# Reordering the last K loads, sharing slots and laying one weight block on 64 partitions in a decode attention kernel

## The chip, the cores and the metric

The kernel runs on one core of a Trainium2 chip. The metric is the time of one execution in microseconds on the device; the figure for a kernel is the median of its runs. Profiles give the "span" of one execution, which is about 2 us shorter than the time. Five engines matter here: PE (matmuls), DVE (transposes and copies), ACT, POOL, and SP, which only issues transfers. The transfers themselves run on 16 DMA engines.

## The reference

One decode step of attention over a KV cache, plus a gated feed-forward part. Cut to what matters:

```
x: 4 x 1 x 1024;  k_cache, v_cache: 4 x 32 x 8192 x 128 (bf16);  wo: 4096 x 1024
q = x @ wq
p = softmax(q @ k_cache^T * Dh**-0.5);  o = p @ v_cache
a = o.reshape(4, 1, 4096) @ wo
out = g * a + (1 - g) * b        # b: feed-forward part; g: a sigmoid gate
```

The caches are 537 of the 576 MB that are read. Everything else is small.

## The kernel before

The caches are read in 64 K pieces and 64 V pieces, each of 4 MB: one transfer to 128 partitions of 32 KB. They go through a ring of five slots, together with the weights. K0 to K63 are followed by the V pieces with a lag of four: K60, V56, K61, V57, and so on. A K piece is transposed on DVE and multiplied on PE; after every fourth, the softmax of a group runs; then four V pieces are multiplied with its result. At the end, wo is read in blocks of 512 rows (1 MB), wo0 to wo7, and multiplied with the heads' outputs (LT). In the profiles, `piece` is a slot of the ring, `o_ps` the product with V, and `acc` the sum to which the wo blocks are added.

```python
ring = ctx.enter_context(tc.tile_pool(name="ring", bufs=5))
def slot():
    return ring.tile([P, RING], BF, name="piece", tag="piece")       # 128 x 32 KB

def wo_piece(g0, g1, r0=0, r1=FR):                                    # a slot for each block
    w = slot()[:, :ng * nr * D].rearrange("p (g r n) -> p g r n", g=ng, r=nr)
    nc.sync.dma_start(out=..., in_=wov[:, g0:g1, r0:r1]...)           # 128 partitions x 8 KB
    def use(): ...  mm_acc(acc[...], LT[:, r0 + r, g0 + g, :], w[:, g, r, ...])
    return use

for u in range(NT + LAG):                                             # NT = 64, LAG = 4
    if u < NT: k_piece(u)
    if u >= LAG: v_piece(u - LAG)
    ...
    if u == NT: o_rows(0, GE); add_x()
    if u == NT + LAG - 2:                                             # after V62
        for g in range(2): wo_piece(g, g + 1)()                       # wo0, wo1
last = [wo_piece(g, g + 1) for g in range(2, NWB - 1)]                # wo2 .. wo6, after V63
last += [wo_piece(NWB - 1, NWB, 0, FR - 1), wo_piece(NWB - 1, NWB, FR - 1, FR)]   # wo7 in two
# ... cuts: V63 is read in four transfers of 1 MB
```

## Time and profile before

| | before |
|---|---|
| time, median (range) | 1351.51 us (1351.25 to 1352.2) |
| span of the profiled run | 1349.4 us |
| DMA engines, mean over the span | 427 GB/s |
| PE busy / DVE busy | 79% / 46% |
| last of the 16 increments of the last wo block | 1345.2 us |
| last matmul ends | 1346.5 us |

From the page of the kernel before: the span, the busy line, and per fortieth of the span the granted PE clock in tenths, the busy tenths of the DMA engines and their GB/s.

```profile
span 1349.4 us, 11817 instructions
PE 1065.0 (79%) x5112; PEld 434.1 (32%) x5112; DVE 622.4 (46%) x403; ACT 71.0 (5%) x118; POOL 86.2 (6%) x326
...
PEclk9877998989899888989989898999988889998999
DMA  9999999999999999999999999999999999999997
GB/s 402 431 433 422 432 431 430 431 432 433 430 431 432 431 428 432 434 430 428 432 434 431 428 432 434 431 429 430 434 431 428 432 434 432 429 429 434 433 421 321
...
HBM read 575.69 MB, written 0.01 MB: 427 GB/s over the span
```

The DMA line reads 9 everywhere but in the last slice, so the kernel is bound by transfers. A mean over 16 engines does not say, however, which of them ends last. The trace also records completion increments (semaphores raised): 16 for each of the transfers below, 4 for the load of x, which has 4 rows (1289.4 to 1294.3 us). I read them as one for each DMA engine that takes part; the map of experiment 1 bears this out. Those of V60 and of the end of wo7, sorted, in the kernel before (us):

```
V60   1287.8 1287.9 1288.2 1289.3 1289.4 1290.0 1290.9 | 1294.0 | 1294.3 1294.3 1295.5 1295.6 1295.6 1295.7 1295.7 1295.8
wo7b  1341.3 1341.3 1341.4 1341.5 1341.5 1341.6 1341.9 | 1343.4 | 1344.7 1344.9 1344.9 1345.0 1345.0 1345.1 1345.1 1345.2
```

Seven engines are early, one is in between and eight are late, by up to 8 us, though early and late ones alike take 9.71 us per 4 MB. The latest increments follow each other every 9.71 us per 4 MB, and then every 2.48 us per 1 MB, without a gap to the end. The late engines set the time. What made them late is not settled: the trace also has 40 instruction fetches of 16 KB, and behind those at 1285.2, 1313.9 and 1337.9 us one late engine each falls back by 1.1 to 1.5 us; for the other 37 this is not shown.

The end of the chain of waits of the kernel before, in order of time (start, duration, what):

```profile
1299.37 8.75 PE o_ps L342 x32
...
1309.47 20.69 DMA piece<-in_A_v_cache_dram
...
1330.21 1.90 PE o_ps L342 x8
...
1332.13 10.53 DMA piece<-in_A_wo_dram
...
1342.69 1.89 PE acc L150 x8
...
1344.59 1.90 PE acc L150 x8
```

wo6 is complete at 1342.65 and wo7a, the first part of wo7, at 1344.55; PE's last two pieces of work start within 0.05 us of that: PE waits for transfers, and has no arrears (work for which everything has long landed). The transfers issued by SP at the end:

```profile
start us, us, engine line op out<-in xcount [idle before <-releaser]
...
1286.55 9.29 SPq L239 DMA_DIRECT2D piece<-in_A_wo_dram  x2
1308.15 1.75 SPq L336 DMA_DIRECT2D piece<-in_A_v_cache_dram  x4
1317.12 21.17 SPq L239 DMA_DIRECT2D piece<-in_A_wo_dram  x7
```

L239 issues the wo blocks; the last seven issues are spread from 1317.12 to 1338.3, because each needs a slot of its own.

### The profile page before, as it was taken

What the parts mean: (1) busy time and instruction counts of PE and PEld (TensorE: products, weight loads), DVE (VectorE), ACT (ScalarE), POOL (GpSimd) and SP (SyncE); (2) the same over time, 40 slices, a digit from 0 to 9 for tenths busy, and PEclk for the clock granted to TensorE, in tenths of its full rate; (3) what the DMA queues carried; (4) which work ended last, traced back from release to release, by engine and by line L of the source; (5) the groups of instructions that cost most, each with busy time, mean ns of one, the idle gap of its engine ahead of it and who ended that gap; (6) DMA issues with size and microseconds to landing.
All of it is one profiled execution on the core that took longest, in us unless ns stands there. A gap on an engine that the chain in (4) does not pass through costs nothing.

```text
span 1349.4 us, 11817 instructions
## 1 busy us (share of the span) xinstructions
PE 1065.0 (79%) x5112; PEld 434.1 (32%) x5112; DVE 622.4 (46%) x403; ACT 71.0 (5%) x118; POOL 86.2 (6%) x326
## 2 busy tenths in 40 slices
PE   2776887778788877868788777879778787887798
PEld 2432333233233323323333323333333333333333
DVE  1553445544544545355355535534553454455420
ACT  0001000000000000000000000000000000000000
POOL 2000000000000000000000000000000000000000
PEclk9877998989899888989989898999988889998999
DMA  9999999999999999999999999999999999999997
GB/s 402 431 433 422 432 431 430 431 432 433 430 431 432 431 428 432 434 430 428 432 434 431 428 432 434 431 429 430 434 431 428 432 434 432 429 429 434 433 421 321
DMA packets 22040, 576.46 MB, mean 427 GB/s; under 512 B 2386, under 2 KB 2394, under 8 KB 2660
## 3 DMA queue, kind: packets, MB, share of 16 engines
q1 hardware_dynamic: 21968, 575.69, 99.4%
q8 instruction: 40, 0.66, 0.2%
q14 instruction: 12, 0.10, 0.0%
q10 hardware_dynamic: 20, 0.02, 0.0%
HBM read 575.69 MB, written 0.01 MB: 427 GB/s over the span
## 4 chain that ended last, share of the span: by engine, by line
DMA 47%; PE 31%; DVE 11%; issue 8%; POOL 2%; ACT 1%; SPq 0%; DVEq 0%; ACTq 0%
DMA piece<-in_A_k_cache_dram 45%; PE o_ps L342 16%; PE S_ps L286 12%; DVE T L279 10%; DMA piece<-in_A_v_cache_dram 2%; PE oT L355 1%; PE acc L150 1%; DMA piece<-in_A_wo_dram 1%; DVE PT L311 1%; POOL PB_143 L316 1%; POOL PB_142 L316 1%; PE shr L150 1%; POOL tot L320 0%; ACT OS_138 L348 0%; ACT OS_139 L348 0%
## 5 line engine op out<-in xcount | busy, mean ns | idle before, releaser
L279 DVE STREAM_TRANSPOSE T<-piece 128x2048 uint32<-128x2048 uint32 x256 | 576.3, 2288 | 477.0 <-DMA piece<-in_A_k_cache_dram 395.1
L286 PE MATMUL S_ps<-T,Z_140 128*128 128x512 bf16 x1024 | 296.5, 447 | 169.0 <-DVE T L279 168.6
L286 PE MATMUL S_ps<-T,Z_141 128*128 128x512 bf16 x1024 | 253.6, 393 | 77.8 <-DVE T L279 77.7
L342 PE MATMUL o_ps<-piece,PB_143 128*8 128x512 bf16 x1024 | 227.1, 381 | 2.3 <-POOL PB_143 L316 2.1
L342 PE MATMUL o_ps<-piece,PB_142 128*8 128x512 bf16 x1024 | 226.2, 379 | 0.0
L286 PEld LDWEIGHTS <-Z_140 128*128 128x128 bf16 x1024 | 113.5, 111 | 347.8 <-issue 272.2
L286 PEld LDWEIGHTS <-Z_141 128*128 128x128 bf16 x1024 | 100.7, 99 | 229.5 <-issue 130.4
L342 PEld LDWEIGHTS <-PB_143 128*8 128x8 bf16 x1024 | 86.5, 87 | 139.8 <-issue 15.6
L342 PEld LDWEIGHTS <-PB_142 128*8 128x8 bf16 x1024 | 86.4, 87 | 137.3 <-issue 13.2
L358 DVE SCALAR_TENSOR_TENSOR OT<-oT,sgb,rinv 128x8 bf16<-128x8 f32 x16 | 3.8, 236 | 128.4 <-PE oT L355 128.4
L270 POOL COPY Z_140<-qa 32x4 bf16<-32x4 bf16 x128 | 24.9, 195 | 512.5 <-PE S_ps L286 497.7
L270 POOL COPY Z_141<-qa 32x4 bf16<-32x4 bf16 x128 | 24.9, 195 | 511.6 <-PE S_ps L286 506.0
L348 ACT COPY OS_138<-o_ps 8x512 f32<-8x512 f32 x32 | 18.4, 576 | 599.7 <-PE o_ps L342 599.7
L348 ACT COPY OS_139<-o_ps 8x512 f32<-8x512 f32 x32 | 18.4, 576 | 536.1 <-PE o_ps L342 536.1
L150 PE MATMUL shr<-xw,piece 128*128 128x4 bf16 x704 | 22.6, 170 | 3.5 <-DMA piece<-in_A_wq_dram 3.3
L150 PEld LDWEIGHTS <-piece 128*128 128x128 bf16 x704 | 22.6, 113 | 4.6 <-DMA piece<-in_A_wq_dram 3.4
L150 PE MATMUL acc<-piece,LT 128*4 128x512 bf16 x64 | 14.6, 378 | 1.1 <-DMA piece<-in_A_wo_dram 1.1
L322 DVE RECIPROCAL rinv<-tot 128x8 f32<-128x8 f32 x16 | 3.2, 202 | 25.5 <-POOL tot L320 25.5
L355 PE MATMUL oT<-selg,OS_139 128*128 128x8 f32 x64 | 8.5, 259 | 5.7 <-ACT OS_139 L348 5.7
L355 PE MATMUL oT<-selg,OS_138 128*128 128x8 f32 x64 | 8.5, 259 | 5.7 <-ACT OS_138 L348 5.7
L316 POOL COPY PB_143<-PT 64x512 bf16<-64x512 bf16 x8 | 8.2, 1026 | 66.0 <-DVE rex L318 66.0
L150 PE MATMUL acc<-piece,hT 128*4 128x512 bf16 x56 | 12.4, 379 | 0.0
(99 smaller groups left out, 145.1 us busy)
## 6 DMA issues: line engine op xcount, KB each, us to landing
piece<-in_A_k_cache_dram SPq DMA_DIRECT2D x64, 4096.0 KB, 37.4
piece<-in_A_v_cache_dram SPq DMA_DIRECT2D x63, 4096.0 KB, 36.5
piece<-in_A_wq_dram SPq DMA_DIRECT2D x2, 4096.0 KB, 22.8
piece<-in_B_w_gate_dram SPq DMA_DIRECT2D x2, 3584.0 KB, 39.6
piece<-in_B_w_up_dram SPq DMA_DIRECT2D x2, 3584.0 KB, 34.5
piece<-in_A_wo_dram SPq DMA_DIRECT2D x7, 1024.0 KB, 14.4
piece<-in_B_w_down_dram SPq DMA_DIRECT2D x1, 4096.0 KB, 39.4
piece<-in_A_v_cache_dram SPq DMA_DIRECT2D x4, 1024.0 KB, 16.7
```

Of the source, the lines that this page charges most:

```text
L150: nc.tensor.matmul(out_ap, lhsT=lhsT, rhs=rhs, start=start, stop=True, skip_group_check=True)
L270: nc.gpsimd.tensor_copy(out=Z[32 * a:32 * a + 32, :, 31 + 32 * a:32 + 32 * a], in_=qa[32 * a:32 * a + 32, :, h0 + a // QH, b:b + 1])
L279: nc.vector.transpose(out=T[:].rearrange("p j h i e -> p (j h i e)").bitcast(U32), in_=kn[:, c * CJ * Dh:(c + 1) * CJ * Dh].bitcast(U32))
L286: nc.tensor.matmul(sps[:, :], lhsT=Z[:, he, s:s + P], rhs=T[:, 16 * jl:16 * jl + 16, half, :, e], start=(t == 0 and jc == 0 and he == 0), ...
L311: nc.vector.transpose(out=PT[:].rearrange("p j i -> p (j i)"), in_=PTs[:])
L316: nc.gpsimd.tensor_copy(out=B_[W:P, :, :, 1, :], in_=Pv[W:P])
L322: nc.vector.reciprocal(out=rinv[:], in_=tot[:])
L342: nc.tensor.matmul(o_ps[32 * t:32 * t + NM, :], lhsT=B_[:, JC * t + jc, uq].rearrange("p s j -> p (s j)"), rhs=vn[:, j0 * Dh:(j0 + 4) * Dh ...
L348: nc.scalar.copy(out=o_sb[32 * t:32 * t + NM, :], in_=o_ps[32 * t:32 * t + NM, :])
L355: nc.tensor.matmul(oT[:, :], lhsT=o_sb[:, q * Dh:(q + 1) * Dh], rhs=selg[:, q].rearrange("p t s -> p (t s)"), start=(q == 0), stop=(q == 3))
L358: nc.vector.scalar_tensor_tensor(out=OT[:, hg:hg + GH, b], in0=oT[:, :], scalar=sgb[:, 1, b:b + 1], in1=rinv_t.pop(g)[:], op0=ALU.mult, op ...
```

## The change

The intent: K61 to K63 are loaded one or two V pieces sooner, so that the last softmax is done well before V60 is there; four wo blocks share a slot, so that they are issued sooner; the load of x and its four matmuls move to the middle of the kernel; and wo0 is laid on partitions 0 to 63, by eight transfers of 8 rows of 16 KB, four before V62 and four after it. The diff, cut to its core:

```diff
+    def wo_half_load(g, p0):
+        if g not in half_w:
+            half_w[g] = slot()[0:P // 2, :2 * FR * D].rearrange("p (s r n) -> p s r n", s=2, r=FR)
+        wv = A_wo[P * FR * g:P * FR * (g + 1)].rearrange("(s p r) n -> p s (r n)", s=2, r=FR)
+        for i in range(4):
+            sl = slice(p0 + i, p0 + 32, 4)                  # 8 partitions, 4 apart
+            nc.sync.dma_start(out=half_w[g][sl]..., in_=wv[sl])
+    def wo_block(g, r0=0, r1=FR):
+        home, at = divmod(g, 4)                             # four blocks in one slot
+        ...
-    for u in range(NT + LAG):  (K_u, V_u-4 in turn to the end)
+    order = ... K59, V55, then K60 K61 V56 K62 K63 V57 V58 V59 V60 V61 V62 V63
+        if (kind, u) == ("v", NT - 2): wo_half_load(0, 0)   # before V62
+        if (kind, u) == ("v", NT - 1):                      # before V63
+            wo_half_load(0, 32)
+            wo_half_use(0)                                  # 16 matmuls of 64 rows
+            wo_block(1)()
 ... (half_rows: the selector matmuls that lay the heads' outputs out for 64 partitions; cut)
```

More of the change, by code (lines that the diff above doesn't have):

```diff
@@ L136 @@
     LT = const.tile([P, FR, H // FR, Bn], BF)
+    LTh = const.tile([P // 2, 2, FR, Bn], BF)
     hT = const.tile([P, FG, FR, Bn], BF)
@@ L234, in o_rows, with half_rows, wo_half_use @@
         nc.vector.tensor_copy(out=LT[:, :, g0:g1, :], in_=lp[:])
-    def wo_piece(g0, g1, r0=0, r1=FR):
-        ng, nr = g1 - g0, r1 - r0
-        w = slot()[:, :ng * nr * D].rearrange("p (g r n) -> p g r n", g=ng, r=nr)
-        nc.sync.dma_start(out=w.rearrange("p g r n -> p g (r n)"),
-                          in_=wov[:, g0:g1, r0:r1].rearrange("p g r n -> p g (r n)"))
+    def half_rows(g):
+        lp = ops.tile([P // 2, 2, FR, Bn], F32, name="o_ps")
+        for k in range(WB):
+            for r in range(FR):
+                k2 = k % 2
+                nc.tensor.matmul(lp[32 * k2:32 * k2 + 32, k // 2, r], lhsT=identb[:, r:P:FR], rhs=OT[:, WB * g + k, :],
+                                 start=True, stop=True, skip_group_check=True)
+        nc.vector.tensor_copy(out=LTh[:], in_=lp[:])
+    half_w = {}
+    def wo_half_load(g, p0):
[4 more added lines that the diff above has]
+            sl = slice(p0 + i, p0 + 32, 4)
+            nc.sync.dma_start(out=half_w[g][sl].rearrange("p s r n -> p s (r n)"), in_=wv[sl])
+    def wo_half_use(g):
+        for s in range(2):
+            for r in range(FR):
+                for n in range(NH):
+                    mm_acc(acc[:, n * NB:(n + 1) * NB], LTh[:, s, r, :], half_w[g][:, s, r, n * NB:(n + 1) * NB])
+    wo_home = {}
+    def wo_block(g, r0=0, r1=FR):
+        home, at = divmod(g, 4)
+        if home not in wo_home:
+            wo_home[home] = slot().rearrange("p (g r n) -> p g r n", g=4, r=FR)
+        w = wo_home[home][:, at]
+        nc.sync.dma_start(out=w[:, r0:r1].rearrange("p r n -> p (r n)"),
+                          in_=wov[:, g, r0:r1].rearrange("p r n -> p (r n)"))
         def use():
-            for g in range(ng):
-                for r in range(nr):
-                    for n in range(NH):
-                        mm_acc(acc[:, n * NB:(n + 1) * NB], LT[:, r0 + r, g0 + g, :], w[:, g, r, n * NB:(n + 1) * NB])
+            for r in range(r0, r1):
+                for n in range(NH):
+                    mm_acc(acc[:, n * NB:(n + 1) * NB], LT[:, r, g, :], w[:, r, n * NB:(n + 1) * NB])
         return use
@@ L369 @@
     GE = NWB - GH // WB
-    for u in range(NT + LAG):
-        if u < NT:
-            k_piece(u)
-        if u >= LAG:
-            v_piece(u - LAG)
-        if side:
+    order = []
+    for u in range(NT - GT):
+        order += [("k", u)] + [("v", u - LAG)] * (u >= LAG)
+    n0 = NT - GT - LAG
+    order += [("k", NT - 4), ("k", NT - 3), ("v", n0), ("k", NT - 2), ("k", NT - 1)]
+    order += [("v", u) for u in range(n0 + 1, NT)]
+    for kind, u in order:
+        if kind == "k":
+            k_piece(u)
+        if (kind, u) == ("v", NT - 1):
+            wo_half_load(0, 32)
+            wo_half_use(0)
+            wo_block(1)()
+        if (kind, u) == ("v", NT - 2):
+            wo_half_load(0, 0)
+        if kind == "v":
+            v_piece(u)
+        if side and (kind == "v" or u < LAG):
             side.pop(0)()
-        if u == NT:
-            o_rows(0, GE)
+        if (kind, u) == ("k", NT // 2):
             add_x()
-        if u == NT + LAG - 2:
-            for g in range(2):
-                wo_piece(g, g + 1)()
-    last = [wo_piece(g, g + 1) for g in range(2, NWB - 1)]
-    last += [wo_piece(NWB - 1, NWB, 0, FR - 1), wo_piece(NWB - 1, NWB, FR - 1, FR)]
+        if (kind, u) == ("v", NT - LAG):
+            half_rows(0)
+            o_rows(1, GE)
+    last = [wo_block(g) for g in range(2, NWB - 1)]
+    last += [wo_block(NWB - 1, 0, FR - 1), wo_block(NWB - 1, FR - 1, FR)]
     flush()
```

## The prediction

> **What bounds the kernel now.** The DMA engines, for the whole span. The page has DMA at 9 tenths or more in every slice but the last (7), 575.69 MB read; the windows view gives 431 GB/s from 100 to 1240 us. PE is busy 79%, DVE 46%. I read the trace's completion increments, one per DMA engine and transfer. Each 4 MB piece has 16, spread over 8 us: seven engines early, one in between, eight late. V60 (V piece 60): 1287.8 to 1290.9 us (seven), 1294.0 (one), 1294.3 to 1295.8 (eight). The latest increments follow each other every 9.71 us, then every 2.48 us per 1 MB block until 1345.2: the late engines never idle. The early seven run dry after 1330, since the last wo blocks are issued at 1332.1, 1336.2 and 1338.0 (timeline of the queue). They end at 1341.3 to 1341.9, the in-between engine at 1343.4, the late eight at 1344.7 to 1345.2. Then comes a fixed tail (last acc matmuls, cast, output transfer), 4.2 us to 1349.4.
>
> So the end is set by the bytes of the last of 16 engines, not by order, slots or PE.
>
> **What the change does.**
> 1. K60 to K63 sooner, wo blocks in shared slots: the same bytes. The last softmax comes about 20 us sooner, wo2 to wo7 are issued by about 1320 instead of 1338. That removes waits of the early seven and of PE, none of which ends last. Worth about 0. I expect no starvation: each slot comes free some 20 us before it is needed.
> 2. wo0 goes to 64 partitions by eight transfers of 8 rows. [...] here engines 0 to 7, each 128 KB instead of 64 KB; 8 to 15 get none. No run has shown it for 8 rows yet. From the trace, 64 KB per engine is 2.48 us. If the late eight are 8 to 15, they end 2.48 us sooner, at about 1342.7.
> 3. But the in-between engine belongs to the lower half. The 8 KB load of x (4 rows[...]) leaves increments at 1289.4, 1290.1, 1291.1 and 1294.3, each just behind one of V60; the last is the in-between engine, only 1.75 us ahead of the latest. It takes 2.48 us more: 1343.4 + 2.5 = 1345.9. It becomes the last, 0.7 us later than now.
> 4. 16 matmuls of 64 rows for 8 of 128, 16 selector matmuls more, one copy more: PE waits for transfers there, so 0.
>
> **Predicted:** 1351.5 + 0.7 = 1352.2 us, range 1350.2 to 1353.4. Chances: faster by over 2% 0.01, within 2% 0.98, slower by over 2% 0.01.
>
> **What will show it.** Increments of the last blocks: the late group some 2.5 us earlier, one single engine last at about 1345.9, the early seven no longer dry, ending near 1341 despite more bytes. wo2 to wo7 issued before about 1325. Tail unchanged at 4.2 us, time per 4 MB at 9.71 us.
>
> **What would make it wrong.** If the in-between engine's lag[...] is smaller in the new order, the gain shows: down to 1349.1. If 8-row transfers land on other engines than 0 to 7, or the late eight are not 8 to 15, up to 2.5 us slower (1354). If the two K pieces in a row leave the queue empty, slower too; then the 9.71 us rhythm breaks between 1230 and 1290.

1343.4 + 2.5 = 1345.9 against 1345.2 is the 0.7 us, and 1351.5 + 0.7 = 1352.2 us. That 8 rows go to engines 0 to 7, and 4 rows to 0 to 3, was an assumption then; experiment 1 shows both, and each small transfer of the change leaves 8 increments.

## The result, and the profile after

| | before | after |
|---|---|---|
| time, median (range, runs) | 1351.43 us (1351.25 to 1352.2, 4) | 1355.44 us (1355.06 to 1356.02, 4) |
| span of the profiled run | 1349.4 us | 1354.3 us |
| V62 complete | 1315.2 us | 1317.5 us |
| last increment of wo7 | 1345.2 us | 1347.3 us |
| last matmul ends | 1346.5 us | 1351.4 us |

The ratio is 1.0029, with a 95% interval of 1.0012 to 1.0046. A ratio here is the mean time of one kernel's fast runs over that of the other's of the same rounds, so it is not quite the ratio of the medians. The change is within 2%, as predicted, but it costs 4.0 us where 0.7 us was predicted (the stated range went up to 1353.4 us).

The page after, the same lines:

```profile
span 1354.3 us, 11866 instructions
PE 1069.8 (79%) x5136; PEld 435.7 (32%) x5136; DVE 622.6 (46%) x404; ACT 71.0 (5%) x118; POOL 86.2 (6%) x326
...
DMA  9999999999999999999999999999999999999996
GB/s 403 429 432 429 426 433 431 432 430 432 431 431 430 431 432 430 430 429 432 431 432 433 429 432 428 431 430 432 431 433 430 432 427 432 431 431 431 432 413 267
```

The GB/s differ by 7 at most in any slice until the last two, where they fall to 413 and 267 (before: 421 and 321), and the DMA line ends in 6 instead of 7. So the loss lies in the last 70 us, with the transfers done before the end. The chain of waits after:

```profile
1283.76 33.76 DMA piece<-in_A_v_cache_dram
...
1317.56 9.67 PE o_ps L374 x32
1327.23 4.71 PE acc L151 x21
...
1332.60 6.06 PE o_ps L374 x29
...
1341.09 10.32 PE acc L151 x47
```

This chain ends otherwise than before. From 1317.56 (V62 is complete) to 1351.4 there is no wait for a transfer at all: V62's 32 matmuls, wo0 and wo1 (4.71 us), V63, and then 10.3 us of acc matmuls in one run. PE is in arrears: it has only short waits for ACT and DVE (0.7 and 0.3 us). It also ran at a lower clock in V62, as the windows view of the kernel after shows (columns: stretch, its length, busy time of the engines, granted PE clock, DMA share, GB/s):

```profile
core 0: us, PE busy (x) PEld busy (x) DVE busy (x) ACT busy (x) POOL busy (x), PEclk, DMA share, GB/s
1304.60:1313.00 8.40, 7.64 (x61) 3.09 (x56) 0.42 (x2) 0.61 (x2) 0.00 (x0) 1.00 0.95 403
1313.00:1317.50 4.50, 0.00 (x0) 0.00 (x0) 0.00 (x0) 0.54 (x1) 0.00 (x0) 0.84 0.95 397
1317.50:1327.20 9.70, 9.64 (x33) 3.23 (x34) 0.00 (x0) 0.00 (x0) 0.00 (x0) 0.72 1.00 411
```

V62's matmuls took 9.67 us at a mean clock of 0.72; at full clock the same 32 take 7.07 us in other places. The clock records have half clock from 1316.0 to 1322.9; it begins while PE stands idle for 4.7 us (1312.9 to 1317.6), waiting for V62. Had V62 taken 7.07 us, PE would have ended at 1351.4 - 2.6 = 1348.8. The transfers alone allow about the same: wo7a is complete at 1346.7, and its and wo7b's eight matmuls take 1.9 us, so 1348.6. By this estimate the 4.9 us of the span divide into about 2.3 us, up to where the later transfers and PE at full clock both end, and 2.6 us that PE, without slack, loses to the lower clock.

The queue after, for the order of issues:

```profile
...
1275.19 3.01 SPq L256 DMA_DIRECT2D piece<-in_A_wo_dram  x4
1283.76 0.34 SPq L368 DMA_DIRECT2D piece<-in_A_v_cache_dram  x1
1286.35 20.82 SPq L256 DMA_DIRECT2D piece<-in_A_wo_dram  x4
1307.28 0.38 SPq L272 DMA_DIRECT2D piece<-in_A_wo_dram  x1
1307.75 10.71 SPq L368 DMA_DIRECT2D piece<-in_A_v_cache_dram  x4
1318.75 11.51 SPq L272 DMA_DIRECT2D piece<-in_A_wo_dram  x7
```

L256 are the eight transfers of wo0, L272 the other wo blocks. wo3 to wo7 are indeed issued sooner (1319.4 to 1329.9; before, 1323.2 to 1338.0); wo2 is not (1318.8; before, 1317.1). The first two rows below are increments of the kernel after for V61 and for the first of the eight small transfers, the last is its final transfer:

```
V61       1297.4 1297.5 1297.7 1298.8 1299.2 1299.4 1300.3 | 1303.5 | 1303.7 1303.7 1305.2 1305.2 1305.5 1305.5 1305.7 1305.8
8 rows    1298.1        1299.4 1299.8 1300.0 1301.0        | 1304.1 | 1304.4 1304.4
wo7b      1339.5 1339.9 1339.9 1340.8 1341.2 1342.0 1342.2 1342.2 1342.3 1342.5 1342.5 1342.8 1342.8 | 1345.5 | 1347.3 1347.3
```

Each increment of the small transfer stands some 0.6 us behind one of V61: five early ones, the in-between one, and two late ones. I had placed all eight late engines outside the lower eight. Two are inside. They got the extra bytes and ended last.

### The profile page after: what moved, and what is told of

It is laid out like the page before. It is cut to its first block, busy times and chain, and to the rows that moved or that the text cites. A ratio compares the mean times of both kernels' runs of the same rounds, so it can differ in the third digit from the quotient of the medians.

```text
span 1354.3 us, 11866 instructions
## 1 busy us (share of the span) xinstructions
PE 1069.8 (79%) x5136; PEld 435.7 (32%) x5136; DVE 622.6 (46%) x404; ACT 71.0 (5%) x118; POOL 86.2 (6%) x326
## 4 chain that ended last, share of the span: by engine, by line
DMA 47%; PE 33%; DVE 11%; issue 6%; POOL 2%; ACT 1%; SPq 0%; DVEq 0%; ACTq 0%
DMA piece<-in_A_k_cache_dram 41%; PE o_ps L374 16%; PE S_ps L318 13%; DVE T L311 10%; DMA piece<-in_A_v_cache_dram 5%; PE acc L151 2%; PE oT L387 1%; DVE PT L343 1%; POOL PB_142 L348 1%; PE shr L151 1%; POOL PB_143 L348 1%; POOL tot L352 0%; ACT OS_139 L380 0%; ACT OS_138 L380 0%; DVE OT L390 0%
## 5 line engine op out<-in xcount | busy, mean ns | idle before, releaser
L341 ACT ACTIVATE PTs<-S_ps,negm 128x512 bf16<-128x512 f32 x16 | 11.0, 687 | 27.4 <-DVE negm L338 27.1
```

The lines of the kernel that those rows point to most:

```text
L341: nc.scalar.activation(out=PTs[:], in_=sps[:], func=ACT.Exp, bias=negm[:, 0:1], scale=scale, accum_out=rs[:, 0:1])
```

## The experiments

Theory A: the loss comes from which engines carry wo0. Two late engines carry 64 KB more (2.5 us); and half of that stands before V62, which delays V62 and puts PE in arrears. Rival B: the new order of K and V pieces costs the time. Rivals C and D and theory E are named where they came up. The runs were made on three chips, four kernels on each, with the kernel before beside them: 1351.20 us (probe, no_half, half_only, half_late), 1351.43 (half_one, half_up, lean, pe_busy) and 1351.34 (pe_busy2 and the extra runs). All of them are within 2% of it. A difference of 2 us is 0.15%, and the intervals reach about as far to either side, so what follows rests on times whose ranges do not overlap and on the increments, not on the ratios.

### 1. A map of the engines

```diff
+ one load of k rows of 64 bytes, k = 1 .. 15, after V41 .. V55, each to its own bytes, read by nobody
```

> The kernel before with 15 small loads of k = 1 to 15 rows of 64 bytes, one after each V piece from 41 on. It maps the engines. Theory A (some of the late engines are among the lowest-numbered eight): the increments of the 8-row load stand behind five early increments, the in-between one and two late ones of the V piece ahead of it, and going from k-1 to k rows adds one engine at a time, so that it can be told which numbers are late; loads of 4 rows show three early and the in-between one. What I predicted (engines 0 to 7 are the seven early and the in-between one): the 8-row load shows no late increment, and loads of 9 rows and more add late ones only. Time as before, 1351.4 us, within 1 us, as the loads carry under 1 KB each.

Measured: one timed run, 1352.3 us. Start times of the small packets, sorted, for some k; successive rows lie 19.44 us apart:

```
k=1                   929.17
k=2                   948.61         948.97
k=3                   968.04         968.41  970.01
k=4                   987.48         987.85  989.44  991.47
k=5                  1006.92 1007.12 1007.30 1008.89 1010.91
k=6                  1026.36 1026.56 1026.74 1028.33 1030.35 1031.33
k=8          1064.05 1065.25 1065.43 1065.62 1067.20 1069.22 1070.15 1070.20
k=9  1083.38 1083.49 1084.76 1084.88 1085.07 1086.65 1088.66 1089.59 1089.64
k=14 two earliest, four early, in-between, then 1186.82 1186.86 1186.97 1187.06 1188.45 1188.49 1188.54
```

Each k adds one engine to those of k-1; an engine is numbered by the row in which it joins, from 0. Row 4 adds the in-between engine (number 3); rows 6 and 7 add late ones (5 and 6); rows 8 and 9 add the two earliest (7 and 8); rows 10 to 15 add late ones only (9 to 14); engine 15 is left and must be the third of the earliest. So engines 5, 6 and 9 to 14 are late, 3 is in between, and the rest are early. My prediction that 0 to 7 hold no late engine falls; theory A's map stands.

### 2. The change without its half block

```diff
-            wo_half_load(0, 32); wo_half_use(0); wo_block(1)()
+            wo_block(0)(); wo_block(1)()
-        if (kind, u) == ("v", NT - 2): wo_half_load(0, 0)
-            half_rows(0); o_rows(1, GE)
+            o_rows(0, GE)
```

> The change without its half block: K pieces sooner and shared slots stay, the first wo block is an ordinary transfer to 128 partitions again, before V63. Theory A (the loss comes from 64 KB more on late engines, and from V62 that lands 2.4 us later behind half of the block, which leaves PE with 34 us of work from 1317.6 on): latest increment of the last wo block back at 1345.2 within 0.6, V62 complete near 1315, time 1351.4 us (1350.8 to 1352.2). Rival B (the new order is at fault: PE waits for V pieces, gets a lower clock after each wait, and ends late): 1354 us or more, the last acc matmul at 1350 or later.

Measured: 1351.10 us (1351.03 to 1351.39), ratio 0.9999 (0.9982 to 1.0016); last increment 1345.1, V62 complete at 1315.4. The end of its chain of waits:

```profile
1294.77 28.04 DMA piece<-in_A_v_cache_dram
...
1322.83 19.77 DMA piece<-in_A_wo_dram
...
1342.64 3.78 PE acc L151 x16
```

PE again waits for the wo transfers before its last 16 matmuls. Rival B falls: the new order and the shared slots cost nothing. They also gain nothing, since the late engines were never idle before. The half block is the whole loss.

### 3. The half block alone, in the old order

```diff
 before.py
+        if u == NT + LAG - 2: wo_half_load(0, 0)          # before V62
-            for g in range(2): wo_piece(g, g + 1)()
+            wo_half_load(0, 32); wo_half_use(0); wo_piece(1, 2)()
```

> The kernel before with the half block alone: old order of the K pieces, a slot for each wo block, four of the eight 8-row transfers before V62 and four after it. Theory A: latest increment of the last wo block at about 1347.3 instead of 1345.2 (two late engines carry 64 KB more), and the time about 1353.6 us (1353.0 to 1354.6), as PE is in arrears from the late softmax and does not stand idle before V62. Rival B: 1351.4 us within 0.5.

Measured: 1354.62 us median, ratio 1.0023 (1.0008 to 1.0038), in two groups: 1353.34 and 1354.09, and 1355.16 and 1355.18. The last increment of the profiled run (the one of 1353.34) is at 1347.1. So 2 us come with two late engines again, and in half of the runs nearly 2 us more; the median lies at the upper edge of what was expected. In the profiled run:

```profile
1310.61 13.94 PE o_ps L370 x64
1324.55 4.71 PE acc L151 x21
...
1338.41 10.32 PE acc L151 x47
```

PE has no gap before V62 here (64 matmuls for V61 and V62 in 13.94 us, full clock), but it is in arrears too: wo0 to V63 and then 10.32 us of acc matmuls without a wait. That part of my expectation, that PE's arrears would not matter here, was too simple; see experiments 9 and 12.

### 4. All eight small transfers after V62

```diff
+            wo_half_load(0, 0)
             wo_half_load(0, 32)                            # both before V63
-        if (kind, u) == ("v", NT - 2): wo_half_load(0, 0)  # none before V62
```

> The change with all eight transfers of the half block behind V62 instead of four on each side: the same bytes on the same engines, V62 sooner. Theory A with its second part (PE's arrears after a late V62 are a cost of their own): V62 complete near 1315 instead of 1317.5, latest increment of the last block 1347.3 as in the change, last acc matmul at about 1348.7 instead of 1351.2, time about 1353.2 us (1352.5 to 1354.2). If the transfers alone set the end: 1355.4 us unchanged.

Measured: 1353.59 us (1353.29 to 1353.85), 1.85 us under the change's median, with the same bytes on the same engines (the change was timed beside other runs of the kernel before; each against its own, 4.0 and 2.4 us, the difference is 1.6 us). V62 is complete at 1315.3, the last increment stands at 1347.6.

```profile
1318.38 14.30 DMA piece<-in_A_v_cache_dram
...
1337.05 12.01 PE acc L151 x47
```

The last 47 matmuls end at 1349.06 (expected: 1348.7). They take 12.0 us instead of 10.3 because the clock records have half clock from 1337.4 to 1340.8, and even so they end only 0.3 us after the transfers allow (wo7a complete at 1346.9, plus 1.9 us): PE has slack again. So V62's delay has a cost of its own, a little under 2 us, on top of the bytes. A side effect that I had not expected: eight issues in a row let the queue run dry. Between 1312.8 and 1315.3 the DMA engines moved 147 GB/s only, and the six late engines outside the lower eight got their next block 3 us late. Those six had 2.5 us to spare.

### 5. Half block by one transfer of 64 rows

```diff
-        for i in range(4):
-            sl = slice(p0 + i, p0 + 32, 4)
-            nc.sync.dma_start(out=half_w[g][sl]..., in_=wv[sl])
+        nc.sync.dma_start(out=half_w[g]..., in_=wv)         # 64 rows, once, after V62
```

> The change with its half block loaded by one transfer of 64 rows after V62 instead of eight transfers of 8 rows: the same partitions, the same 16 matmuls of 64 rows on PE, the same shared slots. [...] Theory A (the loss comes from which engines carry the block): latest increment of the last wo block at 1345.2 within 0.5, time 1351.2 us within 0.7. Rival C (64 partitions alone, with 8 matmuls more on PE, cost something of their own): 1352.5 us or more.

Measured: 1358.54 us (1357.92 to 1358.79), last increment 1352.5. Both expectations miss: the time is 7 us longer. (Theory A's rests on my assumption that each of the 16 engines carries 64 KB of these rows, as of an ordinary block. No figure shows it for 64 rows.) Rival C (64 rows cost PE something) cannot explain it either, since PE is not what made the transfers late. The packets do. Median duration of a packet on the DMA engines, by size, in 1305 to 1310 us:

```
            32 KB packets   8 KB packets   all engines together
before          1215 ns          313 ns         421 GB/s
half_one        1785 ns          645 ns         293 GB/s
```

While these 64 rows are written, 8 KB packets take twice as long, and the 32 KB packets of the neighbouring V pieces half as long again in the median (up to 2512 ns).

### 6. Half block on partitions 64 to 127

```diff
-            half_w[g] = slot()[0:P // 2, ...]
+            half_w[g] = slot()[P // 2:P, ...]               # LTh and its selector matmuls likewise
```

> The change with the half block on partitions 64 to 127 instead of 0 to 63, by the same eight transfers of 8 rows around V62. Theory A (a transfer of 8 rows runs on the lowest-numbered eight engines wherever it writes): as the change, each half transfer's eight increments stand behind five early, the in-between and two late ones of V61, latest increment of the last block at 1347.3, time 1355.4 us (1353.2 to 1356.0). Rival D (the engine goes with the partition): the increments stand behind two early and six late ones, and six engines carry the excess; the in-between one then ends about 1341 instead of 1345.5.

Measured: 1365.08 us (1364.88 to 1365.33), ratio 1.0100. The first small transfer has increments at 1298.6, 1300.0, 1300.4, 1300.7, 1303.6, 1308.3, 1309.7 and 1309.9: again five early, the in-between and two late engines. So the engine goes with the shape of the transfer and not with the partition, against rival D. But the time is 10 us worse than expected, with 8 KB packets at 620 ns and 32 KB packets at up to 2.5 us.

### 7. Another cut of wo0 over the engines

```diff
-  eight transfers of 8 rows, 4 partitions apart
+  rows 48-50, 51-53, 54-56 before V62; rows 0-47, 57-59, 60-62, 63 after it   (3 rows: engines 0 to 2 by the map)
```

> The change with another cut of the first wo block over the engines: 48 of its 64 rows of 16 KB by one transfer[...], 15 rows by five transfers of 3 rows (engines 0 to 2, which the map shows as early; 80 KB each) and one row by itself; three of the small ones before V62, the rest after it. [...] Theory A: latest increment of the last block at about 1344.6 (1345.1 in the kernel before), time about 1350.6 us, 0.6 under the kernel before. Rivals that blame the small transfers as such or the 64 rows: no gain, or 1352 us and more.

Measured: 1363.25 us (1360.23 to 1363.99). It was meant to take 16 KB from each late engine and gain 0.6 us (an estimate from 2.48 us per 64 KB; it assumed that the 48 rows spread evenly over 16 engines, which was not shown); it lost 12 us. Packets are slow again (32 KB: up to 3.5 us).

Runs 5 to 7 have one thing in common that the change lacks: their transfers of wo0 write other partitions at a time. In the change, the 8 rows of one transfer lie 4 partitions apart, on partitions 0 to 63, and 8 KB packets take 312 ns in the median (1300 to 1305 us). half_one writes 64 consecutive partitions by one transfer (645 ns), half_up the upper half (620 ns), and lean 48 and 3 consecutive ones. Theory E: the partitions make the packets slow, and not the bytes of an engine. Experiment 11 tests it. Why these partitions would do so, no run shows.

### 8. Useless matmuls before V62, misplaced

```diff
+        if (kind, u) == ("v", NT - 3):
+            for _ in range(20): mm_acc(shr[0:8, :], identb[:, 0:8], qa[...], start=True)
```

> The change with 20 matmuls of no use (8 columns of an identity with 512 columns, into a bank that nobody reads any more) between V61 and V62 on PE, where it stood idle for 4.7 us: 20 at 0.21 us fill 4.3 us. The transfers are not touched: latest increment 1347.3. Theory A's second part (PE's lower granted clock in V62, 9.67 us for its 32 matmuls where 7.07 are usual, follows from the idle time and is what carries the end from the transfers' end to 1351.4): V62's matmuls take 7.1 us, the last acc matmul ends at about 1348.8, time about 1353.2 us (1352.7 to 1353.9). If the idle time is not the cause of the lower clock, or the matmuls in arrears would not matter: 1355.4 us.

Measured: 1354.39 us median, with runs at 1353.39, 1353.62, 1355.16 and 1355.28. The experiment itself failed: these matmuls depend on nothing recent, and the scheduler moved them to the start of the kernel. In its last 100 us the kernel is the change itself. It is still of use as such: in its profiled run (1353.39) V61's matmuls happened to fall into a stretch of half clock and took 8.76 us, so PE then stood idle for 3.2 us only, V62's took 7.07 us at full clock, and PE ended at 1348.8. The same tail costs 2 us more or less with the clock alone.

### 9. Useless matmuls before V62, in place

```diff
 v_piece(u), behind its own 32 matmuls:
+        if u == NT - 3:
+            for j in range(20): mm_acc(shr[0:8, :], identb[:, 0:8], vn[:, 512 * j:512 * j + 512], start=True)
```

> The change with 20 useless matmuls placed where pe_busy was meant to have them (there the scheduler moved them to the start, so that run was the change itself in its tail): now they read V61's tile, behind or among its own matmuls, and PE has no idle time of 4.7 us before V62. Theory A's second part: V62's matmuls at full clock in every run, 7.1 us, last acc matmul at about 1348.8, all runs at 1353.0 to 1354.0 us and none at 1355. If idle time is not what lowers the clock: runs at 1355 us and above as in the change.

Measured: 1355.11 us median; runs at 1353.51, 1353.54, 1355.11, 1355.40 and 1355.49. No run was to be at 1355, so the expectation missed in part. PE's timeline in the profiled run (1355.11):

```profile
1312.32 3.83 PE L151 MATMUL shr<-piece,identb 128*8 128x512 bf16 x17
1317.56 7.07 PE L374 MATMUL o_ps<-piece,PB 128*8 128x512 bf16 x32 [1.41 <-DMA piece<-in_A_v_cache_dram]
...
1336.76 1.06 PE L390 MATMUL oT<-selg,OS 128*128 128x8 f32 x8 [0.72 <-ACT OS L383]
...
1338.48 11.99 PE L151 MATMUL acc<-piece,LT 128*4 128x512 bf16 x47
```

The useless matmuls fill the gap (1.41 us of idle time are left), and V62 takes 7.07 us as expected. But now the last 47 acc matmuls take 11.99 us: the clock records have half clock from 1338.9 to 1342.3, which costs 1.7 us there. The part of the theory that put the loss on V62's idle time alone falls. What stands is wider: once V62 is late, PE has no slack to the end, and a stretch of half clock anywhere in those 34 us goes straight to the time. Where such a stretch falls differs from run to run. What sets one off is not shown: that of the change began at 1316.0, 3.2 us into an idle time of 4.7 us; that of pe_busy2 had only waits of 0.7 and 0.3 us on PE in the 5 us before it; and the kernel before has one of 3.4 us from 1299.8, behind waits of 0.7 and 2.1 us.

### 10. 64 KB more on engines 0 to 7, and 64 KB more on engines 0 to 2

Both start from experiment 2, which ran like the kernel before, and add loads that nobody reads, after V62:

```diff
+            xs = slot()
+            four transfers of 16 KB rows to xs:  extra8: partitions 0, 4, .. 28 and 1, 5, .. 29, two each
+                                                 extra3: partitions 0, 4, 8 and 1, 5, 9, two each
```

> The change without its half block (which ran like the kernel before), with 64 KB more for each of engines 0 to 7: four loads of 8 rows of 16 KB that nobody reads, behind V62, on partitions 4 apart[...]. Theory A: engines 5 and 6 are late ones and take 2.48 us more: latest increment of the last block at about 1347.4 instead of 1345.1, time 1353.4 us (1352.6 to 1354.4), though no engine carries less than before.

> The same, with four loads of 3 rows: 64 KB more for each of engines 0 to 2, which the map shows as early by 5 us and more[...]. Theory A: latest increment unchanged at 1345.1, time 1351.2 us within 0.7. If the small transfers themselves cost time: 1352.5 us or more.

Measured: extra8 1353.35 us (1353.20 to 1353.46), last increment 1347.4, ratio 1.0014 (1.0000 to 1.0028). extra3 1351.10 us (1350.97 to 1351.25), last increment 1345.0. Both as theory A has it: 64 KB more on each of three early engines are free, 64 KB more on each of a set that holds two late engines cost 2 us. In all extra8 carries more (512 KB against 192 KB), but its last block has two increments at 1347.2 and 1347.4 and none of the others after 1345.4, so two engines and not the sum set the end. In extra8 the chain of waits ends with

```profile
1344.94 3.76 PE acc L151 x16
```

that is, PE starts these matmuls as wo6 is complete at 1344.9. V62 is on time in it, PE waits for transfers, and no run came near 1355.

### 11. The same bytes on the same engines, on other partitions

```diff
-  extra3:      partitions 0, 4, 8 and 1, 5, 9
+  extra3_port: partitions 20, 21, 22 and 52, 53, 54
```

> The same bytes on the same engines 0 to 2, but written to partitions 20 to 22 and 52 to 54[...]. Theory E (half_one, half_up and lean were slow[...]; the packets of 8 KB took 0.62 us there instead of 0.31):[...] latest increment 1349 to 1352, time 1355 to 1359 us. If only bytes per engine counted: 1351.2 us, as extra3.

Cut above are theory E's reason and the sum behind 1355 to 1359 us. The sum came to up to 7 us for one late engine; both rested on which engine writes which partitions in 128-row transfers, and no run shows that.

Measured: 1357.15 us (1356.67 to 1358.49), last increment 1350.8. Against extra3 only the partitions differ, and it costs 6 us. The 8 KB packets in 1310 to 1315 us took 1224 ns in the median against 312 ns in extra3, four times as long; 32 KB packets took up to 4.7 us. The slow packets hold up all late engines: V62 is complete only at 1321.1 (extra3: 1315.3), SP issues the second part of V63 only then, at 1321.15 (extra3: 1315.29), and the other late engines end at 1349.1 to 1349.7 too. Theory E stands as far as that: at equal bytes on equal engines, the partitions made the packets slow. It accounts for the direction of runs 5 to 7; for those three I have not split the loss further.

### 12. What the twelve runs say together on PE's arrears

Times of all runs of kernels in which two late engines carry 64 KB more, on partitions 0 to 63, 4 apart:

```
V62 delayed (four small transfers before it)
  change      1355.06 1355.30 1355.58 1356.02
  half_only   1353.34 1354.09 1355.16 1355.18
  pe_busy     1353.39 1353.62 1355.16 1355.28
  pe_busy2    1353.51 1353.54 1355.11 1355.40 1355.49
V62 on time
  half_late   1353.29 1353.50 1353.67 1353.85
  extra8      1353.20 1353.33 1353.38 1353.46
```

With V62 on time all eight runs lie within 0.7 us. With V62 delayed, 11 of 17 lie at 1355 us and above. (The rows come from different chips; the medians of the kernel before differ by 0.23 us.) The clock records of the profiled runs show a stretch of half clock behind the slow ones (change: 1316.0 to 1322.9; pe_busy2: 1338.9 to 1342.3) and none between 1313 and 1348 in the fast ones (half_only, pe_busy). Only one run of each kernel has a profile, so for the other runs this is argued and not shown.

## Why the prediction was right or wrong

- "The end is set by the bytes of the last of 16 engines" held: extra3 and extra8 show it, and so does the 2.1 us of the change's last increment.
- Point 1 held: order and shared slots are worth 0 (experiment 2). The rhythm of 9.71 us held as well. wo2 to wo7 were issued by 1329.9, not by about 1320, and wo2 no sooner than before.
- Point 2 failed at "if the late eight are 8 to 15". That engines 0 to 7 take an 8-row transfer was right, and that the engines outside them end 2.5 us sooner too (1342.2 to 1342.8 for six of the eight). But the late engines are 5, 6 and 9 to 14. I had inferred the set from one load of 4 rows, which only tells about engines 0 to 3; 4 to 7 were a guess from symmetry. The text named this as a way to be wrong, with up to 2.5 us, and 2.1 us is what it cost.
- Point 3 was right in kind and not decisive: the in-between engine ended at 1345.5 (predicted 1345.9), but two late ones ended at 1347.3.
- Point 4 failed: "PE waits for transfers there, so 0". Half of wo0 before V62 delayed V62 to 1317.5, 2.3 us later than before. PE had 34 us of work left from there, no wait for a transfer in it, and lost 2.6 us more to a lower clock. I had computed when the last transfer lands, and not whether PE would then be free. The 16 matmuls for 8, which point 4 also put at 0, are part of that work: they take 3.61 us (8 of an ordinary block: 1.89), so by this estimate PE would have had some 1.5 us to spare without them. No run has V62 late with 8 matmuls, so how the second loss divides between the delay and these matmuls is not shown; half_late has all 16 and loses little.
- The tail from the last landing was not 4.2 us as predicted but 1354.3 - 1347.3 = 7.0 us, for that reason.

In sums: predicted +0.7 us; measured +4.0 us, of which about 2 come with two late engines (extra8: +2.0) and a little under 2 with V62's delay (half_late against the change: 1.85, or 1.6 with each against its own runs of the kernel before).

No version here beats the kernel before by more than noise: experiment 2 and extra3 equal it. The increments suggest that taking 16 KB from every late engine, on partitions that leave the packets as fast as in the change, would gain about 0.6 us (an estimate, from 2.48 us per 64 KB); with intervals of 0.15% no run could have shown it, so it was not built (lean tried it, and its packets were slow).

## What to carry to other kernels

When a kernel is bound by transfers, read the completion increments engine by engine before moving bytes between engines, and map every engine that the move touches. Look at the packets' durations whenever a small transfer moves to other partitions: with the same bytes on the same engines, 8 KB packets took 312 ns here (extra3) or 1224 ns (extra3_port). And check that whatever consumes the last bytes has slack: here four small transfers placed ahead of V62 made it 2.3 us later (1315.2 to 1317.5 us), and all of PE's work behind it with it.
